# Ten extra products at the start, and six tiles of the last stage in another pool

## The chip, the core and the metric

One core of a Trainium2 chip. TensorE (PE) multiplies, with the loading of its stationary operand shown as a row of its own (PEld); VectorE (DVE) and ScalarE (ACT) do elementwise work and empty PSUM, GpSimd (POOL) makes index tables at the start, SyncE (SP) issues nearly all transfers. The metric is the device time of one execution in microseconds (us), as the median of several runs. A profiled execution also has a span, from its first to its last instruction, and all places below are times from the span's start.

## What is computed

A layer and its gradients: forward and backward of

```python
mod = (silu(c) @ w_mod).reshape(1, 6, 1, 512)      # sa, ca, ga, sb, cb, gb
h = layernorm(x) * (1 + ca) + sa
x = x + ga * irfft2(rfft2(h) * (w_r + 1j * w_i))    # x: 2048 x 512, filters 2048 x 257
h = layernorm(x) * (1 + cb) + sb
x = x + gb * (relu(h @ w1 + b1) ** 2 @ w2 + b2)     # w1: 512 x 1792
```

The outputs are x and, for a given grad_out, the gradients of x, w_r, w_i, w1, b1, w2, b2, c and w_mod, all in bf16.

## The kernel before

The 2048 rows are taken as 16 row tiles of 128 (NT), four to a block. The Fourier transforms are products with tables of sines that the kernel makes itself.

**The stages.** (1) Start, to about 50 us: loads, tables, the modulation rows (`mod_row`, L733), the first norm and the first transform (L294, L295), and between them the products of the gate's gradient, w2T by gT (`back_products`, L837). (2) Filters and inverse transform. (3) Per block of rows the second norm, the dense products (L1009, L1038) and their backward. (4) The gradient of w1 (`grad_w1`, L1283) with the second transform. (5) The last stage, from about 330 us: for each pair of row tiles t = 0, 2, ..., 14 the inverse transform of the gradient (`spec_g2` L372 and L374, `spec_g3` L382) and the first norm's backward (`row_pair`, `row_end`), filled up on PE with the gradient of w2 (`grad_w2`, L1382).

**The order.** It is written out by hand. `ORDER` holds, for each engine, the numbers of its instructions as the program makes them, in the order in which they are to run; `set_order` ties each to the one before. Every engine therefore works through a fixed list, and an instruction that waits holds up all behind it.

**The start around the change.** L714 transposes c (PE, into sm_ps); ACT and DVE make the sigmoid and the column from it. L118 transposes the table TA into TAT, copied by DVE (L120). L748 needs DVE's product sacol (L718) and the load wm_2s. The products of L837 go to two PSUM buffers, mm_0s and mm_1s, that DVE (L839) and ACT (L841) empty in turn. The constant `ones_sq`, 128 x 128 ones, is set by DVE at 0.82 us.

**The last stage, pair by pair.** `row_pair` takes the pair's psY from PE, which ACT copies to gs (L1452); DVE unfolds gs to gh1 (L274 to L278) and makes gn (L1454); ACT writes gn times inv1 back to gs with its row sums (L1456); DVE makes q1 = gh1 times n1 (L1457), the second row sums (jk, L1461) and rr (L1463). `row_end` adds the correction (ACT L1468, DVE L1469, L1471) and stores gs (L1472). PE adds the column sums of gh1 and q1 of all pairs into acc1 (L1439, two pairs late). At the end acc1 is put together (ACT L1490, DVE L1492), spread to all partitions (PE L459) and used for the gradient of w_mod, with the last products of `grad_w2` beside it. n1 and the other rows that a pair needs are loaded by SP (`load_rows3`, L1275, L1276), the transposed hidden rows hn for `grad_w2` by transposing loads (L1202).

**The two pools.** `fp` ("fin2") is made before the last stage. The other, `endp["gm"]`, is made when the last unit of `grad_w1` has been given out, before `row_pair(2)`, in the memory that the pools of stage 4 leave free: among them the one of gw1, whose last tile is stored to the output at L1290. The first writers in that memory wait for all that still used it. So pair 0 has gs, gh1 and q1 in `fp`, and pairs 2 to 14 have them in `endp["gm"]`, with 6, 3 and 3 buffers. The results gw of `grad_w2` (ACT L1383) and hn lie in the same new pool.

Of the kernel before, what the change touches and what calls it, by code (L numbers as in the profile page):

```python
# [11 lines left out]
FP32 = mybir.dt.float32  # L12
BF16 = mybir.dt.bfloat16
# [5 lines left out]
D = 512  # L19
# [8 lines left out]
P = 128  # L28
# [349 lines left out]
def spec_g3(tc, K, Tsb, pool):  # L378

    nc = tc.nc  # L380
    psY = pool.tile([P, D], FP32, name="psY")
    nc.tensor.matmul(psY, lhsT=K["TAT"], rhs=Tsb, start=True, stop=True)  # L382
    return psY
# [57 lines left out]
class GMod:  # L441
# [12 lines left out]
    def emit(self, jc, q, row, pool, ppool, nbuf=2, last=False):  # L454
# [21 lines left out]
ENGINES = {"PE": "PE", "ACT": "Activation", "DVE": "DVE", "POOL": "Pool", "SP": "SP"}  # L476
ORDER = {
    "PE": (
        "0-21 139-142 135-138 26-29 22-25 143-146 86-89 34-35 106 36-37 30-33 151-154 147-150 159-162 38-39 155-158 40-45 167-170 "
        "163-166 46-47 175-178 50-51 171-174 52-53 48-49 183-186 107-110 179-182 90-93 191-194 187-190 58-59 199-202 54-57 "  # L480
        "195-198 60-61 94-97 207-210 62-65 203-206 66-69 98-101 215-218 74-75 70-71 211-214 72-73 76-77 102-105 223-226 78-79 "
        "82-85 80-81 111-126 219-222 303-311 127-134 227-234 312-317 324-325 318-319 235-238 320-321 239-242 322-323 328 326-327 "
        "243-246 329-337 340-343 247-250 338-339 344-351 356-359 352-353 251-254 360 354-355 361-367 372-373 255-258 374-375 "
        "368-371 259-262 376-383 388-389 384-387 390-391 263-266 448-455 460-461 267-270 456-457 462-463 458-459 464-469 271-274 "
        "470-473 476-479 474-475 279-282 480-487 275-278 512-513 500-501 514-515 488-489 502-505 490-491 287-290 492-493 283-286 "
        "494-495 518-521 516-517 506-507 496-497 508-509 498-499 522-523 536-537 524-529 538-539 548-551 510-511 530-531 552-553 "
        "532-535 540-543 554-557 560-561 544-547 558-559 566-569 562-563 570-571 564-565 578-579 572-577 580-583 291-294 585-588 "
        "295-298 589-593 299-302 594-598 392-395 608-611 607 396-399 653-656 612 400-403 666-669 404-407 665 408-411 678-682 "
        "412-415 692-694 416-423 695 599 424-427 600 691 601-604 849 605 850 606 851-852 432-435 428-431 862 440-443 436-439 "
        "863-864 696 613-614 865 615-620 444-447 883-884 861 885-886 584 621-624 641-644 625-640 645-652 657-664 670-677 683-690 "  # L490
        "697-832 841-848 853-856 896-897 866-869 857-860 898-899 870-873 833-840 874-881 891-894 882 887-890 895 901-914 900 "
        "915-928 1053 929-942 1054 943-970 1055-1056 971-1024 1066-1067 1025-1032 1068 1033-1036 1045-1048 1065 1049-1052 1069 "
        "1057-1064 1070-1073 1037-1044 1078-1085 1087-1094 1086 1074-1077 1095-1098 1100-1102 1099 1103 1105-1118 1104 1119-1236 "
        "1249 1237-1240 1253 1257-1264 1250 1265-1268 1251 1254 1269-1272 1252 1281-1284 1327-1333 1297-1304 1255 1241-1248 "
        "1289-1296 1256 1285-1288 1273 1305-1311 1274 1277-1278 1316-1322 1275-1276 1279-1280 1338-1344 1323-1324 1312-1313 1325 "
        "1314 1326 1315 1349-1355 1345-1346 1360-1366 1334-1335 1347 1371-1377 1348 1336 1382-1388 1337 1393-1406 1356 1367-1369 "
        "1357 1370 1358-1359 1407-1420 1378 1389-1390 1379 1391-1392 1380-1381 1437-1450 1425 1421 1426-1427 1422 1451-1464 1428 "
        "1423-1424 1433-1434 1429-1430 1435 1431-1432 1436 1465-1488 1505-1520 1497-1498 1521 1489-1492 1499-1500 1493-1494 "
        "1501-1502 1495 1503-1504 1496 1538-1553 1522-1524 1534-1537 1530-1531 1525 1532-1533 1526-1529 1554-1633 1635-1638 1634 "
        "1639-1641 1643-1644 1642 1647-1666 1683-1684 1645-1646 1685-1688 1695-1696 1667-1682 1691-1692 1689 1693-1694 1690 "  # L500
        "1697-1714 1744-1745 1732 1740-1741 1715-1730 1733 1746-1747 1734 1742-1743 1735-1737 1731 1738-1739 1748-1763 1793-1794 "
        "1781-1785 1789-1790 1786-1787 1791-1792 1780 1788 1795-1796 1764-1779 1829-1834 1841-1842 1835-1838 1843-1844 1839-1840 "
        "1797-1828 1861-1868 1845-1860 1897-1898 1885-1886 1909-1910 1891-1892 1887-1888 1911-1912 1893-1896 1899-1900 1915-1916 "
        "1901-1902 1913-1914 1903-1906 1889-1890 1907-1908 1869-1884 1917-1918 1921-1922 1927-1928 1919-1920 1933-1934 1929-1930 "
        "1923-1924 1939-1946 1925-1926 1931-1932 1935-1938 1951-1954 1975-1978 1957-1958 1955-1956 1947-1948 1963-1964 1959-1960 "
        "1965-1966 1979-1980 1969-1970 1961-1962 1971-1972 1949-1950 1967-1968 1973-1974 1989-2004 1981 1985 1982 1986-1987 1983 "
        "1988 1984 2015-2030 2011 2007-2008 2012 2009 2005 2013 2010 2006 2014 2031-2046 2053 2049-2050 2054 2051 2055 2048 2052 "
        "2047 2056-2072 2079-2080 2073 2083 2081 2084-2086 2082 2074 2087-2102 2125 2120 2126-2127 2129-2130 2119 2128 2131-2132 "
        "2075-2078 2133-2148 2159 2155 2160 2149 2161 2156 2162 2157-2158 2150 2103-2118 2201-2202 2205-2206 2195 2203 2196 "
        "2207-2224 2121-2124 2151-2154 2204 2251 2163-2194 2252-2253 2247 2241 2248 2254 2249 2242 2197-2200 2243-2246 2250 "  # L510
        "2225-2240 2271 2255-2270 2272 2277-2308 2273-2276 2327-2334 2309-2326 2351 2335-2350 2368 2352-2367 2369-2417"
    ),
    "ACT": (
        "0-3 5 4 8 7 6 10 9 13 16-17 12 50 11 51 20 15 52 14 53 18-19 55 54 37-38 56 24 21 23 22 57 27 42 58 30 60 31 59 25-26 44 "
# [78 lines left out]
def kernel(  # L593
# [5 lines left out]
    nc = tc.nc  # L599
# [34 lines left out]
    K = build_basic(tc, constp)  # L634
    mmps = ctx.enter_context(Slots(tc, name="mmps", bufs=2, space=PSUM, side="right"))
# [74 lines left out]
    UT = utcs.tile([P, 4, 16, NT, 8], BF16, name="utcs")  # L710
    scb = gall[:, 0, :].rearrange("p (a q) -> p a q", q=P)
    sacol = p0.tile([P, 3, 4], BF16, name="sacol")
    pv = psM.tile([P, 4], BF16, name="sm_ps", bufs=1)
    nc.tensor.transpose(pv, vrow, K["ident"][0:4, 0:4])  # L714
    K["sig"] = nc.scalar.activation(sigcol, pv, AF.Sigmoid).ins
# [96 lines left out]
    for c, neg in enumerate(((), (1, 3), (1, 2), (2, 3))):  # L812
        fs, co = slice(P * c, P * c + P), (0, 3, 1, 2)[c]
        for i in range(4):
            k = int(i in neg)
# [377 lines left out]
    gm = GMod(tc, K, scf, gsc, wm_view, out9_view)  # L1193
    hnp = Slots(tc, name="hnp", bufs=1, side="right")
    hns, endp = [], {}
# [213 lines left out]
    fp = Slots(tc, name="fin2", bufs=2, side="right")  # L1409
# [22 lines left out]
    with Slots(tc, name="psE", bufs=2, space=PSUM) as psE, Slots(tc, name="psS1", bufs=1, space=PSUM) as psS1:  # L1432
# [4 lines left out]
        def colsums1(t, gh1, q1):  # L1437
            for q, row in ((0, gh1[:, 0, :]), (32, q1[:, 0, :]), (64, gh1[:, 1, :]), (96, q1[:, 1, :])):
                nc.tensor.matmul(acc1[q:q + 32, :], lhsT=K["ones_q"], rhs=row, start=(t == 0), stop=(t == NT - 2), tile_position=(0, q))  # L1439
# [3 lines left out]

        def row_pair(t, Ts):
            n1, gxl = rows3[t]
            gh1, q1 = [(endp["gm"].tile([P, 2, D], BF16, name=x, bufs=3) if "gm" in endp else fp.tile([P, 2, D], BF16, name=x, bufs=2)) for x in ("gh1", "q1")]
            gn = fp.tile([P, 2, D], BF16, name="gn")
            gs = (endp["gm"].tile([P, 2, D], BF16, name="gs", bufs=6) if "gm" in endp else fp.tile([P, 2, D], BF16, name="gs", bufs=2))
            rr = fp.tile([P, 2, 4], FP32, name="rr")
            for i in range(2):  # L1450
                psY = spec_g3(tc, K, Ts[i], psE)
                nc.scalar.copy(out=gs[:, i, :], in_=psY)  # L1452
            unfold(nc, fp, gh1, gs, 2, "unf_u")
            nc.vector.tensor_tensor(gn, gh1, modb[:, CA1_B, None, :].broadcast_to([P, 2, D]), op=ALU.mult)  # L1454
            for i in range(2):
                nc.scalar.activation(gs[:, i, :], gn[:, i, :], AF.Copy, scale=inv1[:, t + i:t + i + 1], accum_out=rr[:, i, 0:1])  # L1456
            nc.vector.tensor_tensor(q1, gh1, n1, op=ALU.mult)  # L1457
            late.add(lambda: colsums1(t, gh1, q1))
            for i in range(2):
                jk = fp.tile([P, D], BF16, name="jk1", bufs=1)  # L1460
                nc.vector.scalar_tensor_tensor(out=jk, in0=gs[:, i, :], scalar=K["onef"], in1=n1[:, i, :], op0=ALU.mult, op1=ALU.mult,  # L1461
                                               accum_out=rr[:, i, 1:2])
            nc.vector.tensor_scalar(rr[:, :, 2:4], rr[:, :, 0:2], -1.0 / D, None, op0=ALU.mult)  # L1463
            return t, n1, gxl, gn, gs, rr
# [91 lines left out]
```

## Time and profile before

| | us |
|---|---|
| median of 3 runs | 408.25 (406.55 to 409.12) |
| the profiled execution | 408.54 |
| its span | 406.8 |
| PE busy in the span | 382.3 (94%) |
| DVE busy | 341.8 (84%) |
| ACT busy | 278.4 (68%) |
| DMA queue q1, share of 16 engines | 89.1% |

A line of the timeline gives start, length, engine, line of the kernel, operation, output and input tiles, and in brackets the idle time of the engine before it with what ended it. "x4" is four instructions in one line. In the list of waits a line reads: who waited, for whom, total us, times, longest. In the table by stretches each engine has busy us and number of instructions, then the granted clock of PE (1.00 is full), the DMA engines' share and GB/s. The chain of work that ended last is followed back from the last instruction.

### The profile page before, as it was taken

What the parts mean: (1) busy time and instruction counts of PE and PEld (TensorE: products, weight loads), DVE (VectorE), ACT (ScalarE), POOL (GpSimd) and SP (SyncE); (2) the same over time, 40 slices, a digit from 0 to 9 for tenths busy, and PEclk for the clock granted to TensorE, in tenths of its full rate; (3) what the DMA queues carried; (4) which work ended last, traced back from release to release, by engine and by line L of the source; (5) the groups of instructions that cost most, each with busy time, mean ns of one, the idle gap of its engine ahead of it and who ended that gap; (6) DMA issues with size and microseconds to landing.
All of it is one profiled execution on the core that took longest, in us unless ns stands there. A gap on an engine that the chain in (4) does not pass through costs nothing. (4 is left out here: it accounts for less than half of the span.)

```text
span 406.8 us, 6919 instructions
## 1 busy us (share of the span) xinstructions
PE 382.3 (94%) x2394; PEld 200.9 (49%) x2418; DVE 341.8 (84%) x831; ACT 278.4 (68%) x501; POOL 14.1 (3%) x56
## 2 busy tenths in 40 slices
PE   0998999999999999999999999899999997899996
PEld 0354566665444444444444444465555663444445
DVE  5998979969896799889898999937889874498995
ACT  4568899879870685279536766458576544798795
POOL 4420100000000000000000000000000000000000
PEclk9999999999999999999999999999999999899999
DMA  9999999487594789789877889969999999999997
GB/s 257 250 192 284 224 194 283 151 197 260 166 209 124 203 212 203 173 174 235 196 207 178 181 223 233 260 186 298 294 257 299 244 314 146 228 256 204 246 257 247
DMA packets 141643, 90.97 MB, mean 224 GB/s; under 512 B 95778, under 2 KB 127528, under 8 KB 141096
## 3 DMA queue, kind: packets, MB, share of 16 engines
q1 hardware_dynamic: 140900, 89.93, 89.1%
q10 hardware_dynamic: 708, 0.59, 0.5%
q8 instruction: 19, 0.31, 0.3%
q14 instruction: 16, 0.13, 0.1%
HBM read 36.35 MB, written 33.19 MB: 171 GB/s over the span
## 5 line engine op out<-in xcount | busy, mean ns | idle before, releaser
L1283 PEld LDWEIGHTS <-h_sb 128*128 128x128 bf16 x256 | 24.7, 98 | 22.4 <-issue 1.5
L1038 PEld LDWEIGHTS <-gab 128*128 128x128 bf16 x224 | 21.5, 98 | 25.0 <-DVE gab L1016 0.6
L1009 PEld LDWEIGHTS <-w 128*128 128x128 bf16 x224 | 21.3, 98 | 25.0 <-issue 1.7
L837 PEld LDWEIGHTS <-w2T 128*128 128x128 bf16 x224 | 21.2, 98 | 22.3 <-issue 2.9
L1283 PE MATMUL mm_0s<-gab,h_sb 128*128 128x384 bf16 (+1 forms) x160 | 30.2, 342 | 0.9 <-ACT gw_1s L1288 0.9
L1038 PE MATMUL og_0s<-w1T,gab 128*128 128x512 bf16 x110 | 25.7, 379 | 0.4 <-DVE gab L1016 0.3
L1038 PE MATMUL og_1s<-w1T,gab 128*128 128x512 bf16 x108 | 25.3, 379 | 0.2
L336 ACT ACTIVATE AE<-psB 128x1024 bf16<-128x1024 f32 x16 | 22.2, 1387 | 2.6 <-PE psB L332 2.6
L1009 PE MATMUL mm_1s<-h2T,w 128*128 128x512 bf16 x84 | 21.6, 379 | 0.0
L1283 PE MATMUL mm_1s<-gab,h_sb 128*128 128x512 bf16 (+1 forms) x96 | 20.8, 370 | 0.0
L1009 PE MATMUL mm_0s<-h2T,w 128*128 128x512 bf16 x80 | 20.5, 379 | 0.0
L372 PEld LDWEIGHTS <-utcs 128*128 128x128 bf16 x128 | 10.3, 97 | 13.0 <-issue 6.7
L837 PE MATMUL mm_1s<-gT_0s,w2T 128*128 128x512 bf16 x56 | 15.5, 394 | 0.7 <-DMA w2T<-in_B_w_dram 0.6
L837 PE MATMUL mm_0s<-gT_0s,w2T 128*128 128x512 bf16 x56 | 15.2, 396 | 0.9 <-DMA w2T<-in_B_w_dram 0.6
L1382 PE MATMUL mm_0s<-g_sb,hn_1s 128*128 128x512 bf16 x62 | 15.9, 412 | 0.1
L1009 PE MATMUL pst<-h2T,w 128*128 128x512 bf16 x60 | 15.4, 379 | 0.0
L841 ACT CAST gab<-mm_1s 128x512 bf16<-128x512 f32 x20 | 12.4, 622 | 4.0 <-PE mm_1s L837 3.9
L837 PE MATMUL mm_1s<-gT_1s,w2T 128*128 128x512 bf16 x56 | 14.4, 379 | 0.1
L837 PE MATMUL mm_0s<-gT_1s,w2T 128*128 128x512 bf16 x56 | 14.4, 379 | 0.1
L1382 PE MATMUL mm_1s<-g_sb,hn_0s 128*128 128x512 bf16 (+1 forms) x63 | 12.7, 352 | 0.1
L332 PEld LDWEIGHTS <-utcs 128*128 128x128 bf16 x128 | 9.3, 97 | 4.9 <-issue 1.8
L839 DVE CAST gab<-mm_0s 128x512 bf16<-128x512 f32 x12 | 8.2, 686 | 3.5 <-PE mm_0s L837 3.5
(657 smaller groups left out, 1041.1 us busy)
## 6 DMA issues: line engine op xcount, KB each, us to landing
w<-in_B_w_dram SPq DMA_DIRECT2D x2, 1792.0 KB, 8.0
Z<-wz_dram SPq DMA_DIRECT2D x4, 514.0 KB, 4.1
Xb<-xs_dram SPq DMA_DIRECT2D x4, 514.0 KB, 6.3
x_sb<-in_A_x_dram SPq DMA_DIRECT2D x2, 1024.0 KB, 6.3
n_dram<-x_sb SPq DMA_DIRECT2D x4, 512.0 KB, 4.4
h_dram<-h2r SPq DMA_DIRECT2D x8, 256.0 KB, 2.3
h_sb<-h_dram SPq DMA_DIRECT2D x4, 512.0 KB
g_sb<-in_grad_out_dram SPq DMA_DIRECT2D x2, 1024.0 KB
```

What stands on the lines that cost most here:

```text
L332: nc.tensor.matmul(ps[:, hh, P * co:P * co + P], lhsT=UT[:, c, 2 * gi + hh, :, :], rhs=K["Cd"][:, P * c:P * c + P], start=not extra, stop= ...
L336: nc.scalar.activation(dst, ps.rearrange("p r (s e f) -> p (r s) e f", s=2, e=2), AF.Copy, scale=EF_S)
L372: nc.tensor.matmul(ps[:, P * i:P * i + P], lhsT=CS[:, t, i].rearrange("p a b -> p (a b)"), rhs=K["Cf"][:, i, :], start=True, stop=True)
L837: nc.tensor.matmul(ps, lhsT=w2T[:, dc, fc * P:(fc + 1) * P], rhs=gT[b][:, :, dc, :], start=(dc == 0), stop=(dc == 3))
L839: nc.vector.tensor_copy(out=gaT[b][:, fc, :], in_=ps)
L841: nc.scalar.copy(out=gaT[b][:, fc, :], in_=ps)
L1009: nc.tensor.matmul(ps, lhsT=w1[:, dc, (fc + i) * P:(fc + i + 1) * P], rhs=h2T[b][:, :, dc, :], start=(dc == 0), stop=(dc == 3))
L1038: nc.tensor.matmul(ps, lhsT=lhs(fc), rhs=rhs[:, fc, :], start=(fc == 0), stop=(fc == NFC - 1))
L1283: nc.tensor.matmul(blocks(ps, fb), lhsT=h2_sb[:, t, dc * P:(dc + 1) * P], rhs=gh_rows(t, fb), start=(t == 0), stop=(t == NT - 1))
L1382: nc.tensor.matmul(ps[:, 0:w], lhsT=hns[fc][:, t, :], rhs=g_sb[:, t, c:c + w], start=(t == 0), stop=(t == NT - 1))
```

## The change

Two edits. The first puts ten 128x512 products of `ones_sq` with itself into the buffers mm_0s and mm_1s, in PE's order right behind the transposition of c and ahead of L118; nothing reads their results. The second has pairs 2 and 4 take gh1, q1 and gs from the older pool `fp`, where gs now has three buffers; pairs 6 to 14 take theirs from `endp["gm"]` as before. In `ORDER` only PE's list changes: its start, and by ten each number behind it. The lists of ACT, DVE, POOL and SP are the same.

```diff
 ORDER = {
     "PE": (
-        "0-21 139-142 135-138 26-29 22-25 143-146 86-89 34-35 106 36-37 30-33 151-154 147-150 159-162 38-39 155-158 40-45 167-170 "
+        "10 0-3 5 4 7 6 9 8 11-31 149-152 145-148 36-39 32-35 153-156 96-99 44-45 116 46-47 40-43 161-164 157-160 169-172 48-49 "
...
     sacol = p0.tile([P, 3, 4], BF16, name="sacol")
+    for k in range(10):
+        ps = mmps.tile([P, 4, P], FP32, name="mm")
+        nc.tensor.matmul(ps, lhsT=K["ones_sq"], rhs=K["ones_sq"][:, None, :].broadcast_to([P, 4, P]), start=True, stop=True)
     pv = psM.tile([P, 4], BF16, name="sm_ps", bufs=1)
     nc.tensor.transpose(pv, vrow, K["ident"][0:4, 0:4])
...
         def row_pair(t, Ts):
             n1, gxl = rows3[t]
-            gh1, q1 = [(endp["gm"].tile([P, 2, D], BF16, name=x, bufs=3) if "gm" in endp else fp.tile([P, 2, D], BF16, name=x, bufs=2)) for x in ("gh1", "q1")]
+            gh1, q1 = [(endp["gm"].tile([P, 2, D], BF16, name=x, bufs=3) if "gm" in endp and t >= 6 else fp.tile([P, 2, D], BF16, name=x, bufs=2)) for x in ("gh1", "q1")]
             gn = fp.tile([P, 2, D], BF16, name="gn")
-            gs = (endp["gm"].tile([P, 2, D], BF16, name="gs", bufs=6) if "gm" in endp else fp.tile([P, 2, D], BF16, name="gs", bufs=2))
+            gs = (endp["gm"].tile([P, 2, D], BF16, name="gs", bufs=6) if "gm" in endp and t >= 6 else fp.tile([P, 2, D], BF16, name="gs", bufs=3))
```

## The prediction

> **What bounds the kernel now.** I read the page's slices first: PE is at nine tenths or more in nearly every slice, so a cut elsewhere counts only where PE waits for it. Then I listed what PE, ACT and DVE waited for, by stretch. Two places answer to the two edits.
>
> The waits between 335 and 370 us (who waited for whom: total us, times, longest):
>
> ```profile
> DVE unf_u L274 <- ACT gs_0s L1452: 6.7, 2, 5.2
> ACT gs_0s L1452 <- DMA out_dram<-gw_1s: 4.4, 1, 4.4
> PE psY_0s L382 <- ACT gs_0s L1452: 4.0, 1, 4.0
> ```
>
> One store holds all three engines: ACT cannot write the second row pair's gs until the last gw1 store (L1290) has landed, because that gs lies in the new pool, in memory that the store still reads. DVE waits for ACT's copy, PE for the PSUM tile that the copy would free. The stretches confirm it (busy us of each engine, then granted clock, DMA share, GB/s):
>
> ```profile
> core 0: us, PE busy (x) PEld busy (x) DVE busy (x) ACT busy (x) POOL busy (x), PEclk, DMA share, GB/s
> 342.00:346.00 4.00, 0.81 (x6) 0.35 (x4) 0.13 (x2) 0.00 (x0) 0.00 (x0) 1.00 1.11 136
> 346.00:350.00 4.00, 3.11 (x14) 1.46 (x15) 0.76 (x2) 3.80 (x8) 0.00 (x0) 0.74 0.99 212
> ```
>
> From 342 to 346 nothing computes but the DMA engines; then the granted clock drops. ACT's order there:
>
> ```profile
> 341.24 0.57 ACT L374 ACTIVATE Tsb_1s<-psT_1s 128x512 bf16<-128x512 f32 x1
> 346.20 0.58 ACT L1452 CAST gs_0s<-psY_0s 128x512 bf16<-128x512 f32 x1 [4.39 <-DMA out_dram<-gw_1s]
> 346.68 0.59 ACT L1452 CAST gs_0s<-psY_1s 128x512 bf16<-128x512 f32 x1
> 347.25 0.59 ACT L1452 CAST gs_1s<-psY_0s 128x512 bf16<-128x512 f32 x1
> 347.73 0.59 ACT L1383 CAST gw_0s<-mm_1s 128x512 bf16<-128x512 f32 x1
> ...
> 349.64 0.76 ACT L1456 ACTIVATE gs_0s<-gn_0s,inv 128x512 bf16<-128x512 bf16 x1
> ...
> 352.94 0.58 ACT L1383 CAST gw_1s<-mm_0s 128x512 bf16<-128x512 f32 x1 [2.45 <-PE mm_0s L1382]
> 353.42 1.52 ACT L1468 ACTIVATE gn_0s<-n_0s,rr_0s 128x512 bf16<-128x512 bf16 x2
> ```
>
> The chain that ended last shows what the end hangs on: DVE and ACT in turn from 366 to 390, then PE alone.
>
> ```profile
> 389.52 0.59 DVE acc_sb L1492
> 390.12 0.04 issue
> 390.16 0.39 PE mm L459
> ```
>
> From 390.16 PE has 13.0 us of products to 403.16, and 3.6 us follow to the span's end. So the time is that of the acc1 sum (L1492) plus 16.6 us.
>
> The early edit lies here (PE's timeline):
>
> ```profile
> 8.47 0.29 PE L118 MATMUL sm_ps<-ident,TA 128*128 128x128 bf16 x1 [4.30 <-ACT TA L114]
> ...
> 15.12 1.88 PE L837 MATMUL mm_0s<-gT_0s,w2T 128*128 128x512 bf16 x4
> ...
> 21.69 1.04 PE L837 MATMUL mm_0s<-gT_0s,w2T 128*128 128x512 bf16 x4 [0.57 <-DMA w2T<-in_B_w_dram]
> ...
> 33.96 1.02 PE L733 MATMUL mod_ps<-wm_2s,gab 128*128 128x512 bf16 x3 [1.44 <-DMA wm_2s<-in_w_mod_dram]
> ```
>
> Four equal products take 1.88 us at 15.12 and 1.04 at 21.69, so PE runs at half clock in between 10 and about 16.8 us.
>
> **Edit 1, ten products on ones.** Added: ten 128x512 matmuls and weight loads, between the transposition of c (L714, 4.02) and that of TA (L118, 8.47). At the half clock's step, (1.88 - 0.60)/3 = 0.43 us, they take 4.3 us; one pair uses the same PSUM buffer twice running and waits about 0.2 us for its first half. Start 4.2, end about 8.7: L118 comes 0.2 us late. Behind L118, DVE's queue holds the copy of TAT (L120, 8.82) and all after it; POOL and ACT take theirs from DVE. DVE's next idle time is 0.90 us before 23.63, so 0.2 us is gone there. Without that cover it would reach PE ahead of 33.96, where PE waits 1.44 us for a load anyway.
>
> What they may bring: the Trainium skill, "TensorE: Matmul & The Clock Gate", Part 1 (the HAM clock gate), says PE runs at half clock until a window of about 3.4 us has been busy. By that rule ten idle-time products have the clock up by 10 us, and the twelve 128x512 products between 10.57 and 16.8 save 12 x 0.21 = 2.5 us; the sum would be 2.5 us lower. The rows say otherwise, first of the time (half clock lasts from 10.15 to some 16.8 here, 6.6 us and not 3.4), then of its worth: PE waits for w2T at 21.69 and, 1.44 us, for wm_2s at 33.96, a load that SP issued at 27.48 behind transposing loads and that no PE work triggers. An earlier PE waits longer there. After 33.96 PE is dense to 67. I take 0 (bounds: 0.2 us lost; 2.5 gained if loads moved too, which nothing here does). If that cover were gone the 2.5 us would count.
>
> **Edit 2, gh1, q1 and gs of pairs 2 and 4 into the older pool.** No instruction is added or removed; the built order of ACT, DVE and SP is the same, and so are SP's waits. The set of DMA waits moves on ACT from the copy at 346.20 to the first other writer of the new pool, the gw_0s copy (347.73), three places later; DVE's moves to pair 6 (long landed), PE's to a weight load at 364. New reuse waits (gh1 and q1 of pair 4 on pair 0's column sums) fall at about 352, when those sums (353.71 now, then 349.3) are done.
>
> The new ACT schedule, with the rows' durations: three copies 341.72, 342.20, 342.74 (each 0.48); then gw_0s waits as before to 346.2. PE meanwhile does the psY and psT products by 343.4 and the mm_0s group, 16 x 0.217 = 3.46, to 346.9, at full clock. ACT after 346.2: gw_0s, two Tsb, the fourth copy (0.48 to 0.5 each), L1456 at 348.2 instead of 349.64 (-1.45), gw_1s at 348.9, as PE is no longer late (352.94, -4.0). DVE's jk (0.68), gh half (0.34) and rr (0.08) behind L1456 end at 350.2, and L1468 starts at 350.3 instead of 353.42: **-3.1 us**. From there ACT and DVE hand work to each other in the same steps, so 3.1 stays on their chain. PE itself gains more (4.0 of stall and 1.7, half of one 3.4 us half-clock window) but has to wait for ACT's copies: about 1.7 us before 348.3 and 0.9 at 353. The row at 33.96 says that a 1.44 us idle does not cost the clock.
>
> What is late next: SP. It is filled with transposing loads, and the rows n1 of pairs 12 and 14 come late in its queue:
>
> ```profile
> 377.25 2.03 SPq L1202 DMA_TRANSPOSE hn_5s<-h_dram  x1
> 379.38 0.52 SPq L1275 DMA_DIRECT2D n_0s<-n_dram  x1
> ...
> 381.06 0.34 SPq L1275 DMA_DIRECT2D n_1s<-n_dram  x1
> ```
>
> n_0s lands 3.6 us after its issue, 382.98; DVE uses it (L1457) at 383.36: only 0.4 us of slack. SP between 353 and 379 is idle about 0.35 us before wmc_1s (354.50), 0.4 before n_1s (362.94), which waits for ACT, and 0.85 before hn_0s (367.94), which waits for PE; these 1.6, and some 0.2 in small pieces, are all it can gain. So n_0s lands 1.8 earlier, 381.2, when DVE, 3.2 earlier, is ready at 380.1. DVE waits 1.1 and goes on **2.1 us** early. n_1s (waits for ACT's L1468, so SP-bound at 379.1, plus 4.4 = 383.5) is just in time for 385.84 - 2.1 = 383.7. L1492 ends 2.1 early; PE reaches L459 in time. hn_5s, used at 383.46, is issued 1.8 earlier too and lands 4.3 to 7.1 us after that.
>
> The sum: 0 + 2.1. Span 406.8 to 404.7; the profiled execution 408.54 (1.7 around the span) to 406.4; from the median of 408.25: **406.2 us**. Bounds: SP gains nothing, and only its 0.4 of slack is left; loads keep pace, 3.2.
>
> **The rivals.**
> The DMA engines are the limit. Their share is 0.93 to 1.28 in every stretch from 350 to 394, and they worked through the stall. Then n_0s lands when it does now: gain 0.4, 407.9. Against: they moved 334 GB/s at 386 to 390, and 163 to 299 in the stretches from 354 to 386.
> The loads do not bind: SP's transposing issues, 2.0 to 5.2 us long, shorten when stores are spread differently. Gain 3.2, 405.0.
> The early clock counts as well: needs PE, not the load, to end the wait at 33.96, against that row. 2.1 + 2.5 = 4.6, 403.7.
> Slower: the ten products run late and hold L118, and with it DVE's queue. DVE absorbs 0.9 us at 23.6, PE 1.44 at 33.96, edit 2 repays 2.1: it is slower only if they hold L118 by over 4.4 us, over 0.87 us for each. Nothing near that row: a half-clock step is 0.43, and a strict wait of each for the end of the one before would be about 0.65 (0.60 and a hand-over), 2.2 us late in all, which is hidden. By 0.3 us a product more it would be 3 us slower, 411.
>
> **How the numbers follow.** Likeliest (SP's n1 loads take back a third, gain 1.2 to 2.8): 0.55. DMA-limited (0 to 1.2): 0.22. Loads keep pace (2.8 to 4): 0.13. Early clock counts: 0.06. Slower: 0.04. The three runs of before spread over 2.6 us, so about 1%, 4.1 us, is what a measurement can tell from no change. Over 1% faster takes the early clock or the top of the third case: 0.09; slower by over 1%: 0.04; the rest, 0.87. The range 404.2 to 408.2 holds the first three cases, some 0.85 of it left after the runs' own spread; the likeliest alone is 405.4 to 407.0.
>
> **What would show it.** Right: ACT's wait for out_dram<-gw_1s moves to L1383 and shrinks from 4.4 to about 2.9; no half-clock window near 348; L1468 about 3 us earlier; DVE waits about 1 us for n_dram before L1457 late in the stage. At the start: products at 16 us at full clock, but PE's wait for wm_2s longer than 1.44. Wrong: the DMA wait stays over 4 us elsewhere on ACT; PE goes past 33.96 earlier; a new half-clock window appears in the tail.

## The result and the profile after

| | us |
|---|---|
| kernel before, median of 9 runs | 407.47 (406.44 to 410.03) |
| changed kernel, median of 9 runs | 405.56 (404.55 to 406.58) |
| ratio, with its 95% interval | 0.9949 (0.9929 to 0.9969) |
| profiled execution of the changed kernel, its span | 405.56, 403.8 |

The change made the kernel 1.9 us faster, half a per cent. The forecast was 2.1 us on a median of 408.25: 406.2. A second set of runs of the changed kernel gave 0.9963 (0.9944 to 0.9982), 1.2 us. So the size was about right. The two profiled executions differ by 3.0 us of span, more than that, and the first thing to do is to see what of it belongs to the change.

**The store's wait** moved and shrank. The waits of the changed kernel between 335 and 370 us (who waited for whom: total us, times, longest; its lines are those of the kernel before plus 4, so L1387 copies gw, L1456 copies gs, L1460 and L1472 are the two steps behind it):

```profile
ACT gw_0s L1387 <- DMA out_dram<-gw_1s: 2.2, 1, 2.2
...
PE psY_0s L382 <- ACT gs_0s L1456: 0.2, 1, 0.2
```

The wait for the store is now in front of the copy of gw_0s, 2.2 us instead of 4.4 in front of the copy to gs; PE's 4.0 us wait for that copy is 0.2. ACT's timeline shows the first and the last of the three copies to gs that went ahead of the wait, and what came behind it:

```profile
340.01 0.57 ACT L1456 CAST gs_1s<-psY_0s 128x512 bf16<-128x512 f32 x1
...
341.17 0.59 ACT L1456 CAST gs_2s<-psY_0s 128x512 bf16<-128x512 f32 x1
343.96 0.59 ACT L1387 CAST gw_0s<-mm_1s 128x512 bf16<-128x512 f32 x1 [2.20 <-DMA out_dram<-gw_1s]
...
345.87 0.75 ACT L1460 ACTIVATE gs_0s<-gn_0s,inv 128x512 bf16<-128x512 bf16 x1
...
348.02 1.52 ACT L1472 ACTIVATE gn_0s<-n_0s,rr_0s 128x512 bf16<-128x512 bf16 x2 [0.83 <-DVE rr_0s L1467]
```

The stretches agree (busy us of each engine, then granted clock, DMA share, GB/s): PE has 3.35 us of work between 342 and 346, where it had 0.81, and the clock stays full, where it had fallen to 0.74.

```profile
342.00:346.00 4.00, 3.35 (x16) 1.41 (x15) 0.00 (x0) 2.04 (x5) 0.00 (x0) 1.00 1.03 164
346.00:350.00 4.00, 3.94 (x26) 1.96 (x26) 3.22 (x10) 3.17 (x8) 0.00 (x0) 1.00 1.49 203
```

**Later in the stage** DVE waits for the rows n1 of pairs 10, 12 and 14, 1.07, 1.54 and 0.31 us, where it had waited for none. Its timeline with the first two, and the acc1 sum, in the changed kernel:

```profile
373.99 0.75 DVE L1465 SCALAR_TENSOR_TENSOR jk<-gs_2s,onef,n 128x512 bf16<-128x512 bf16 x1 [1.07 <-DMA n<-n_dram]
...
380.44 0.69 DVE L1461 TENSOR_TENSOR q_0s<-gh_0s,n_0s 128x1024 bf16<-128x1024 bf16 x1 [1.54 <-DMA n_0s<-n_dram]
...
386.92 0.68 DVE L1496 TENSOR_TENSOR acc_sb<-acc,acc_odd 64x512 bf16<-64x512 f32 x1
```

and the acc1 sum in the kernel before:

```profile
389.43 0.68 DVE L1492 TENSOR_TENSOR acc_sb<-acc,acc_odd 64x512 bf16<-64x512 f32 x1
```

The chain that ended last, which had been DVE and ACT in turn from 366 to 390, now runs through SP's queue (SPq) and one of these loads:

```profile
374.53 2.21 SPq L1206
378.42 4.78 DMA n_1s<-n_dram
```

**What belongs to the change.** I took three points of each trace: E, where the stage of pairs begins (DVE's first L274, 336.53 before and 334.83 after); R, where the first `row_end` begins (ACT's first L1468, 353.42, and L1472, 348.02); S, where the acc1 sum begins (L1492, 389.43, and L1496, 386.92). E itself differs by 1.7 us, before either kernel has reached edit 2. Two waits for transfers that only the kernel before has come ahead of it: PE's for wm_2s (1.44 us at 33.96), and ACT's for an earlier gw1 store at about 307 (2.0 us); at 296 us, between the two, the changed kernel is 0.9 us ahead. Between the other traces E moves as much, 334.5 to 336.3, whatever their edits. What the change did in the last stage is read from E to R and from R to S. Behind S the forecast took a fixed time; it is not quite fixed, so the table has it too.

| trace | E | E to R | R to S | S to the end |
|---|---|---|---|---|
| before | 336.53 | 16.89 | 36.01 | 17.3 |
| edit 1 alone | 336.27 | 17.00 | 36.01 | 16.8 |
| before, rows early | 335.93 | 17.18 | 36.02 | 17.3 |
| before, plain loads | 335.43 | 17.73 | 36.01 | 17.3 |
| changed | 334.83 | 13.19 | 38.91 | 16.9 |
| changed, second run | 335.35 | 13.68 | 38.49 | 16.8 |
| edit 2 alone | 335.08 | 13.06 | 37.74 | 17.5 |
| changed, more ones | 335.93 | 12.85 | 37.85 | 16.8 |
| changed, rows early | 334.47 | 13.62 | 37.35 | 17.5 |
| changed, rows early, second run | 335.08 | 13.15 | 35.96 | 17.7 |
| changed, plain loads | 334.55 | 12.88 | 35.96 | 16.8 |

Without edit 2, E to R takes 16.9 to 17.7 us; with it 12.9 to 13.7: **4.0 us gained** (17.2 less 13.2, the means). R to S is 36.0 where nobody waits for a load, to 0.06 us in six traces; in the four traces with edit 2 and the loads as they were it is 37.7 to 38.9, 38.25 in the mean: **2.25 us given back**. The difference, 1.75, is what the change did up to S; from the traces whose loads are as they were it is 1.5 (16.95 less 13.2, and 2.25 given back). The 3.0 us between the two traces are thus 1.7 from the place of E, 3.7 less 2.9 between E and S, and 0.5 behind S.

### The profile page after: what moved, and what is told of

The parts are those of the page before. It is cut to its first block, busy times and chain, and to the rows that moved or that the text cites. A ratio compares the mean times of both kernels' runs of the same rounds, so it can differ in the third digit from the quotient of the medians.

```text
span 403.8 us, 6936 instructions
## 1 busy us (share of the span) xinstructions
PE 385.1 (95%) x2403; PEld 201.8 (50%) x2428; DVE 341.9 (85%) x831; ACT 278.3 (69%) x501; POOL 14.0 (3%) x56
## 4 chain that ended last, share of the span: by engine, by line
PE 64%; DVE 12%; ACT 8%; SPq 7%; DMA 6%; issue 2%; DVEq 0%; ACTq 0%
PE og_0s L1042 8%; PE og_1s L1042 8%; PE mm_0s L1287 6%; PE mm_1s L1287 5%; PE mm_1s L1386 4%; PE mm_1s L841 4%; PE mm_1s L1013 4%; PE mm_0s L1386 3%; PE mm_0s L841 3%; PE mm_0s L1013 3%; DMA w2T<-in_B_w_dram 3%; PE pst L1013 2%; SPq L1206 2%; SPq L693 2%; ACT AE L336 2%
## 5 line engine op out<-in xcount | busy, mean ns | idle before, releaser
L1287 PE MATMUL mm_0s<-gab,h_sb 128*128 128x384 bf16 (+1 forms) x160 | 30.2, 342 | 0.0
L1386 PE MATMUL mm_0s<-g_sb,hn_1s 128*128 128x512 bf16 x62 | 14.2, 379 | 0.1
L1386 PE MATMUL mm_1s<-g_sb,hn_0s 128*128 128x512 bf16 (+1 forms) x63 | 12.7, 352 | 0.1
L407 ACT ACTIVATE inv<-l_mv_1s,eps 128x2 f32<-128x2 f32 x4 | 1.2, 304 | 15.0 <-DVE l_mv_1s L952 15.0
```

The source lines that it names most:

```text
L407: nc.scalar.activation(dst, var, AF.Sqrt, bias=K["eps"])
L1287: nc.tensor.matmul(blocks(ps, fb), lhsT=h2_sb[:, t, dc * P:(dc + 1) * P], rhs=gh_rows(t, fb), start=(t == 0), stop=(t == NT - 1))
L1386: nc.tensor.matmul(ps[:, 0:w], lhsT=hns[fc][:, t, :], rhs=g_sb[:, t, c:c + w], start=(t == 0), stop=(t == NT - 1))
```

## The experiments

**Each edit by itself.** Edit 1 alone has the lines of `row_pair` as they were; edit 2 alone has no extra products and PE's old list (its lines are one lower, L1386 for L1387).

```diff
 edit 1 alone
-endp["gm"].tile(...) if "gm" in endp and t >= 6 else fp.tile(...)
+endp["gm"].tile(...) if "gm" in endp else fp.tile(...)
 edit 2 alone
-    for k in range(10):
-        ps = mmps.tile([P, 4, P], FP32, name="mm")
-        nc.tensor.matmul(ps, lhsT=K["ones_sq"], ...)
```

> Edit 1 alone (the ten products; the tiles of pairs 2 and 4 in the new pool as before). Theory (worth nothing): the same as the kernel before within 0.4 us, about 407.5; the products near 16 us at half clock again, as in the changed kernel's trace; ACT's wait for out_dram<-gw_1s at the first copy to gs, about 4 us. Rival (the changed kernel passed its wm_2s row 0.95 us earlier than the kernel before, and edit 1 is what did it): about 1 us faster, 406.5, and no wait for wm_2s at 33 us.

> Edit 2 alone (no extra products). Theory: it holds the whole gain, 1.9 us, 405.6; ACT's wait for out_dram<-gw_1s at the gw_0s copy and 2 to 3 us; no half clock near 346 us; DVE waits 1 to 3 us for n_dram between 370 and 384. Rival (half of the gain is edit 1's): 406.5.

Edit 1 alone: 406.76 against 406.78, ratio 0.9984 (0.9960 to 1.0007): nothing that can be measured, though the ratio itself stands at 0.6 us and its interval reaches to 1.6. Edit 2 alone: 405.47 on the same chip, 0.9972 (0.9946 to 0.9997), 1.3 us. The waits between 335 and 370 us of edit 1 alone are those of the kernel before:

```profile
PE psY_0s L382 <- ACT gs_0s L1456: 3.8, 1, 3.8
ACT gs_0s L1456 <- DMA out_dram<-gw_1s: 3.7, 1, 3.7
```

and of edit 2 alone, between 335 and 392 us, those of the changed kernel:

```profile
ACT gw_0s L1386 <- DMA out_dram<-gw_1s: 1.9, 1, 1.9
...
DVE q_0s L1460 <- DMA n_0s<-n_dram: 1.3, 1, 1.3
```

Edit 1's trace also passes wm_2s without a wait, at 32.93. But then it waits 1.1 us for the next of these loads, wm_1s, and at 300 us it is 0.26 us behind the trace of before. Edit 2 alone waits only 0.8 us for wm_2s, with no extra products at all. What the last stage gains up to S comes with edit 2 and not with edit 1, as the table shows: 17.00 and 36.01 with edit 1 alone, 13.06 and 37.74 with edit 2 alone.

The rival is not out altogether. PE passes its wm_2s row at 33.4 to 34.0 us in the four traces without the extra products and at 32.2 to 33.4 in the ten with them, though E, some 300 us later, no longer shows the difference. And S to the end takes 17.3 to 17.5 us without them, but 16.8 to 17.0 in eight of the ten traces with them; the two with early rows have 17.5 and 17.7. The difference lies behind ACT's last store: from its issue to the end 3.1 us before, 2.6 in the changed kernel, 2.5 with edit 1 alone and 3.2 with edit 2 alone. Why is not shown. So edit 2 holds the larger part, and some half a microsecond of edit 1's is neither shown nor excluded.

**More ones.** Eight more products behind L118 fill PE's idle time ahead of L752.

```diff
-    for k in range(10):
+    for k in range(18):
 ORDER["PE"]: the last eight behind L118
```

> The changed kernel with eight more products of ones behind L118, where PE is idle for 1.67 us before L752. Theory (the early clock is worth nothing): the clock stays full from about 7.5 us on, the products from 10.8 to 17 us take half the time, PE waits that much longer for w2T and wm_2s, and the time is the changed kernel's, 405.6 within 0.4. Rival (the early clock counts): 2 to 2.5 us less, 403.3.

405.2, ratio 0.9966 (0.9937 to 0.9996): as edit 2 alone, 0.9972. In the changed kernel the clock had risen at about 7.5 us, and fell again. Its stretches (PE's busy time first, the clock third from the end):

```profile
7.50:11.00 3.50, 1.58 (x21) 0.79 (x20) 3.50 (x14) 1.49 (x4) 0.42 (x2) 0.99 1.21 232
11.00:17.70 6.70, 5.75 (x16) 1.78 (x15) 6.70 (x28) 3.00 (x5) 4.66 (x13) 0.50 1.14 271
```

From 7.5 to 11 us, with the last of the ten products in it, PE had 1.58 us of work, and it ran the next 6.7 us at 0.50: the four products near 15 us took 1.91 us, no less than before (1.88 at 15.12). With eight more products it does not fall:

```profile
13.17 1.27 PE L841 MATMUL mm_1s<-gT_0s,w2T 128*128 128x512 bf16 x3 [1.13 <-DMA w2T<-in_B_w_dram]
...
15.07 1.02 PE L841 MATMUL mm_0s<-gT_0s,w2T 128*128 128x512 bf16 x4
```

The same four products take 1.02 us at 15.07, and the time is not lower: PE only waits more, 1.13 us for w2T and 0.41 for DVE. So the early clock does not bring the 2 to 2.5 us of its rival; by these intervals a gain much under 1 us could not be told from nothing.

**Rows early.** What gives back 2.25 us? The changed kernel's list for SP was altered so that the n1 loads of pairs 10, 12 and 14 go out sooner; everything else is the same. The same alteration was also made to the kernel before.

```diff
 ORDER["SP"], the part that is altered:
-hn_0s(transposing) gxl_1s n hn_1s(transposing) gw_4s hn_5s(transposing) n_0s gs_0s gw_6s n_1s
+n hn_0s(transposing) gxl_1s n_0s hn_1s(transposing) gw_4s hn_5s(transposing) n_1s gs_0s gw_6s
```

> The changed kernel with three loads of n1 moved up in SP's list: that of pair 10 ahead of one transposing load, that of pair 12 ahead of two, that of pair 14 ahead of two stores. Theory (their place in SP's queue gives back what edit 2 won): DVE's waits for n_dram, 1.07 + 1.54 + 0.31 us in the changed kernel, go, and the acc1 sum comes 2 to 2.9 us earlier: 402.7 to 403.6. Rival (the DMA engines are the limit, whatever the order): the waits move to the other loads, gain under 0.5: 405.1 to 405.6.

> The changed kernel with the three n1 loads moved up, once more, beside the changed kernel on one chip. Theory (their place in SP's queue counts once edit 2 is in): 1 to 2 us faster than the changed kernel. Rival (its gain was the chip's or chance): the same within 0.4 us.

> The kernel before with the three n1 loads moved up as in the run with early rows, and neither edit. Theory (these loads are late only once edit 2 has brought DVE ahead; before they had 0.4 us of slack): 406.8 within 0.4, as the kernel before. Rival (their place costs the kernel before as much as the changed one): 1.7 us faster, 405.1.

On the changed kernel: 403.78, ratio 0.9941 (0.9917 to 0.9965), and the second time 404.21, 0.9942 (0.9919 to 0.9964). The changed kernel itself, beside the second run, had 405.62 and 0.9963 (0.9944 to 0.9982): 1.4 us between the medians, 0.9 by the ratios, and the two intervals overlap.

> The changed kernel once more, beside the runs with plain loads and the early rows on one chip. Both theories: about 2 us faster than the kernel before (ratio 0.995).

On the kernel before: 0.998 (0.9954 to 1.0007), no difference that can be measured; R to S is 36.02, as without the move. So these loads are late only once edit 2 has brought DVE ahead. The second trace of the changed kernel with early rows shows DVE without a wait for them:

```profile
378.13 0.68 DVE L1461 TENSOR_TENSOR q_0s<-gh_0s,n_0s 128x1024 bf16<-128x1024 bf16 x1
...
384.19 0.68 DVE L1496 TENSOR_TENSOR acc_sb<-acc,acc_odd 64x512 bf16<-64x512 f32 x1
```

The sum begins at 384.19 and R to S is 35.96: up to S all is kept. The first trace keeps less (37.35); there the next load in the queue has become late, PE waiting 1.6 us for hn_5s, and DVE still waits 1.2 us for n_1s.

This version is the fastest of the complete kernels that were run, about 2.4 us below the kernel before. Of what it wins up to S it loses some 0.75 us behind S (17.5 and 17.7 for 16.8 and 16.9). And DVE is no longer what the end hangs on: in the second trace the larger pieces of the chain that ended last are all PE's from 353 us on. The first and the last of them:

```profile
353.14 3.62 PE mm_1s L1386 x16
...
396.34 1.76 PE mm_0s L1386 x16
```

**Plain loads.** The transposing loads that stand ahead of n1 in SP's list were made plain, in the changed kernel and in the kernel before. These two kernels leave the transposition out, so their gradient of w2 is not the right one; bytes and number of loads are the same.

```diff
-nc.sync.dma_start(hns[fc], h_dram[fc, :, :], transpose=True)
+nc.sync.dma_start(hns[fc], h_dram[fc, :, :], transpose=True) if fc in (0, 1, 2, 3, 5) else nc.sync.dma_start(hns[fc], h_dram[fc, :, :].rearrange('p (t q) -> p t q', q=P))
```

> The changed kernel in which the nine loads of hn issued after 346 us are plain instead of transposing: as many bytes and issues, but about 0.5 us of SP each instead of 2 to 5 (PE's products of the gradient of w2 then work on untransposed rows, so out_6 is not the gradient). Theory (edit 2 brings the chain of ACT and DVE 3.1 to 3.7 us forward and only the transposing loads take part of it back): no wait of DVE for n_dram, 3.1 to 3.7 us faster than the same loads in the kernel before, and about 3.3 us faster than the kernel before. Rival (something other than these loads takes it back): about 2 us, as in the changed kernel.

> The kernel before with the same nine plain loads of hn (out_6 is not the gradient). Theory (before the change these loads held nobody up): the kernel before within 0.5 us. Rival (the transposing loads cost the kernel before too): 1 us faster or more.

The changed kernel: 402.45, ratio 0.9898 (0.9876 to 0.9921). The kernel before: 406.98 against 406.86, ratio 1.0003 (0.9985 to 1.0021). So with plain loads the change is worth 4.5 us (E to R 17.73 and 12.88, and nothing given back from R to S), more than the 3.1 to 3.7 expected. With the transposing loads it is worth 1.2 to 1.9. In the kernel before the transposing loads cost nothing that can be measured. SP's timeline of the changed kernel with plain loads:

```profile
366.20 0.42 SPq L1206 DMA_DIRECT2D hn_5s<-h_dram  x1
366.73 0.94 SPq L1279 DMA_DIRECT2D n_0s<-n_dram  x1
```

and of the changed kernel:

```profile
374.53 2.21 SPq L1206 DMA_TRANSPOSE hn_5s<-h_dram  x1
376.85 0.52 SPq L1279 DMA_DIRECT2D n_0s<-n_dram  x1
```

The same load of hn_5s holds the queue 2.21 us or 0.42.

**Queue or engines.** Three more runs asked whether what is scarce is SP's time or the DMA engines. Seven gw stores were issued by GpSimd instead of SP, with and without the early rows; and in a third kernel, stores of the stage were cut to 8 columns.

```diff
 stores by GpSimd
-nc.sync.dma_start(out6_view[:, fc, c:c + w], gw[:, c:c + w])
+(nc.gpsimd if fc in (0, 1, 2, 3, 4, 6, 7) else nc.sync).dma_start(out6_view[:, fc, c:c + w], gw[:, c:c + w])
 small stores
+z = 8 if fc in (0, 1, 2, 3, 4, 6, 7) else w      # gw;  z = 8 if t in (2, 6) else D for gs
```

> The changed kernel with seven gw stores of the last stage issued by GpSimd instead of SP; the bytes are the same and the n1 loads keep their places. Theory (SP's queue): pair 12's load is issued 2.2 us earlier, pair 14's 2.6 us earlier, DVE's waits for n_dram shrink by that, 404.0. Rival (the DMA engines are the limit, SP's transposing loads only lengthen by what is taken from its queue): 405.1 to 405.6.

> The changed kernel with the three n1 loads moved up as in the run with early rows, and seven gw stores of the last stage issued by GpSimd instead of SP. Theory (what holds the stage is the time that SP's queue takes): with 2.6 us less in that queue hn_5s comes earlier, PE's wait of 1.6 us for it goes, 402.3. Rival (DMA engines are the limit): as with early rows alone, 403.8 within 0.4.

> The changed kernel in which seven gw stores and two gs stores of the last stage write 8 columns instead of all (the rest of these rows of out_6 and out_1 is left out): 1.4 MB less for the DMA engines before 386 us, and just as many issues for SP. Rival (the DMA engines are the limit): the ten transposing loads of SP between 338 and 392 us, 37.9 us of issue time in the changed kernel, fall below 34, the n1 loads come 2 us or more earlier, 404 or less. Theory (SP's queue, whatever the engines carry): 37 us or more, 405.1 to 405.6.

These ran on a chip where the kernel before took 410.0, not 406.8, so only ratios can be set beside the others, and the changed kernel was not run there. Their traces are not in the table: E to R 14.0, 13.6 and 14.1, R to S 39.8, 42.5 and 38.7, in the order below. Stores by GpSimd: 0.9984 (0.9958 to 1.0011). With the early rows as well: 1.0020 (0.9991 to 1.0049), where the early rows alone had given 0.994. Small stores: 0.9936 (0.9914 to 0.9958). Neither theory had expected a loss from GpSimd's stores. The nine transposing loads from hn_0s at about 347 us to hn_3s at about 388 hold SP, in sum: 27.1 us before, 26.3 with edit 1 alone, 27.6 in the kernel before with early rows (on this slower chip); 30.3 in the changed kernel, 29.6 in its second trace, 29.8 with edit 2 alone, 29.3 with more ones; 30.0 and 29.0 with early rows; 32.5 and 31.9 with stores by GpSimd; 28.4 with small stores. So in the traces with GpSimd's stores, what was taken off SP's list came back as longer transposing loads. With small stores the ten loads that its expectation counts took 37.4 us, where the theory of the queue had 37 or more and that of the engines less than 34; the changed kernel, on another chip, has 37.9. The next lines are SP's timeline with stores by GpSimd:

```profile
376.89 3.23 SPq L1206 DMA_TRANSPOSE hn_5s<-h_dram  x1
380.22 0.52 SPq L1279 DMA_DIRECT2D n_0s<-n_dram  x1
```

n_0s goes out at 380.22, later than the changed kernel's 376.85, with less in the queue ahead of it. This trace is 1.3 us later at E, and on another chip; the rest is in the transposing loads. What remains open is whether GpSimd's stores themselves lengthen them or the chip does, since no trace of the changed kernel from that chip was taken; and what the small stores' ratio would be beside it.

## Why the prediction held, step by step

**Edit 1, worth 0: right within what can be measured, by its cover and not by its mechanism.** The ten products ran from 4.11 to 8.23 in the changed kernel (forecast 4.2 to 8.7) and L118 stood at 8.47, where it was; with edit 1 alone at 8.56. The step that failed is "products at 16 us at full clock, but PE's wait for wm_2s longer". They were at half clock (1.91 us for four), because PE's 1.67 us without work behind L118 came after (with work put there the clock stayed up), and the wait for wm_2s was not longer but gone. PE's lines of the changed kernel:

```profile
10.37 0.54 PE L752 MATMUL sm_ps<-sacol,wm_2s 128*128 128x1 bf16 x16 [1.67 <-DVE sacol L722]
...
15.34 1.91 PE L841 MATMUL mm_0s<-gT_0s,w2T 128*128 128x512 bf16 x4
...
33.01 1.03 PE L737 MATMUL mod_ps<-wm_2s,gab 128*128 128x512 bf16 x3
```

I had set the trace's 6.6 us of half clock against the rule of the Trainium skill, "TensorE: Matmul & The Clock Gate", Part 1, as if they differed. They need not: the rule speaks of windows of about 3.4 us that run on their own, and the clock here rose, fell and rose at about 7.5, 10.9 and 17.8 us, 3.4 and 6.8 us apart. How much work a window needs the traces do not settle. Nor do the other executions say what the early clock is worth. Their mean granted clock is 1.000 also with edit 2 alone, where the clock rises late, because the slow start is not in that row; and the executions of the changed kernel at 0.999 or 1.000 took 405.56 and 405.91 us in the first set, in its middle, but 403.13, 404.14 and 404.70 in the second, where they are the three fastest of twelve.

**Edit 2's first term, 3.1 us at L1468: measured 4.0, and 3.7 in the two traces compared here.** The order of events was as forecast: three copies ahead of the wait, the wait at gw_0s, PE's group at full clock, gw_1s without its 2.45 us for PE. From L1456 to L1468 the forecast had 1.65 us of its 3.1, and the traces show 1.63 (2.07 us earlier against E at L1460, 3.70 at L1472). The rest was short by 0.6 us: the store's wait ended 9.1 us behind E, not 9.7 as in the trace of before, so it shrank by 2.2 us and not by 1.5.

**Edit 2's second term, 1.0 us given back: measured 2.25.** The mechanism was the one named, n1 of pairs 12 and 14 late in SP's queue behind transposing loads; pair 10's n1, which the forecast did not look at, was late too (1.07 us). The mis-sized term is "these 1.6, and some 0.2 in small pieces, are all it can gain". From the issue of hn_0s (349.19, now 346.77) to that of n_0s SP's queue took 30.2 us before and 30.1 after: its idle time shrank by 1.0 us and its other issues by 1.2, but the seven transposing loads among them took 22.4 us instead of 20.3. So n_0s went out 2.53 us earlier, of which 1.7 had come with E: 0.8 where the forecast had 1.8. Over all nine loads the sum is 27.0 us in the mean of three traces without edit 2 and 29.7 of four with it. The forecast had moved the loads at their old lengths; what lengthened them is not shown. The rival that would have gained 3.2, in which these issues "shorten when stores are spread differently", had the sign wrong.

**The sum** was 2.1 from 3.1 and 1.0; it is 1.75 from 4.0 and 2.25. Both terms were about 1 us short, with opposite signs: that the total came so near is in part luck. The 16.6 us that the forecast put behind the sum, unchanged, moved by half a microsecond as well. The rival of the DMA engines (gain 0.4) forecast less than any set of runs of the changed kernel gave. In part it may be right, since the transposing loads became longer in the tighter stage. The small stores speak against it, but the changed kernel to set beside them on their chip is missing.

## What to carry to other kernels

Measure a change between two points of its own stage before comparing totals: here R to S was 36.0 in every trace in which nothing waited, to 0.06 us, while the place at which the stage began moved by 2 us between executions. A stall taken away in front of a full queue can be given back by the queue: when the engines go faster, look up what each will need next and where its load stands in the issuing queue, and move that load in the same edit (0.9 to 1.4 us more here, for a change of three places in a list). A load of long issue is not of fixed length: in a tighter stage it may hold its queue longer. And a total that agrees says little where two terms of opposite sign are off: compare each.

## What the runs showed of the hardware that was not expected

A transposing load of 512 KB held SP 2.0 to 5.2 us, the plain load of the same bytes 0.33 to 0.43. The first is not a fixed time: nine of them took 27 us in the slack stage, 30 in the tighter one, 32 with GpSimd's stores (these on the slower chip).

Ten products, 4.1 us of work, raised PE's clock at 7.5 to 9.6 us in seven of the nine traces that have them; in the other two, edit 1 alone and stores by GpSimd, it rose only at 16.5 and 17.1. In the changed kernel the clock's changes lie whole steps of 3.41 us apart (7.53, 10.94, 17.77), and where these steps fall differs from trace to trace; which share of a step must be filled is not shown. A stretch with 1.58 us of work in 3.5 was enough to lose the clock again, with no gap longer than 1.67 us. The trace of before gives a granted clock of 1.00 for 10 to 18 us although its products there took twice their time; the row shows the falls, not the slow start.
